# Gathering the tiled products of a linear-attention block: fewer tiled groups, full-array spreads of the reciprocals, scatter pairs, early x loads

## Chip, cores and metric

One core of a Trainium2 chip. The metric is the device time of the kernel in microseconds (us), as the median of several executions. The span that a profile shows is some 1.7 us shorter than that time.

## The reference

Two branches and two residuals are added. x has 2048 tokens of width 640.

```python
xn = layernorm(x)
# branch A: linear attention, 32 heads of width 20
q, k, v = split(xn @ wqkv)
pq, pk  = phi(q), phi(k)              # phi(t) = t+1 if t>0 else exp(t)
kv  = sum over tokens of pk (x) v     # per head, 20 x 20
z   = sum over tokens of pk           # per head
o   = (pq @ kv) / (pq @ z + 1e-6)     # per token and head
A   = o @ wo
# branch B: the 8 tokens of highest x @ w_r go through a gated MLP (640 -> 1536 -> 640);
# the result, times a sigmoid of the score, is added to those 8 rows of x
out = x + A + x + scatter(B)
```

## The kernel before

It first runs over 16 tiles of 128 tokens: layernorm, a transposed copy of the normalised tile (by TensorE for tiles 0 to 3, by a transposing DMA from tile 4 on), the key product K, the phi function, and the Gram product G of the normalised tile with phi(k). Then it turns G into a matrix M = kv·wo (640 x 640), computes the queries in four blocks of 512 tokens, divides them by the denominators, and makes the output tiles as phi(q)/den times M. The routing and the small MLP are threaded between the query products.

What matters for the change is how the small products use TensorE. A product with only 32 output rows is *column-tiled*: four of them, written to four partition ranges of 32, run side by side. A product with only 8 or 32 contraction rows is *row-tiled*: four of them at four partition ranges, written to different PSUM banks, run side by side. All others use the full array. PSUM is one tile of 8 banks, `PS[:, bank, 512]`.

```python
def loads(t):                       # x tiles 6..15, two at a time, on SyncE's DMA queue
    if t < 5:
        ld(sp, XX[:, 6 + 2*t : 8 + 2*t, 1, :], x_v[:, 6 + 2*t : 8 + 2*t, :])
    ...
    # loads(0) follows the first layernorms; loads(1), (2), (3) stand between the transposing
    # DMAs of tiles 4, 5, 6 on the same queue

def m_main(m, b, eng):              # one of 5 slices of M
    for h in range(2):
        for g in range(NG):         # column-tiled, 8 products of 320 columns
            pe.matmul(PS[32*g : 32*g+32, b+h, 0:HW], lhsT=by5(kv1[:, g, :])[:, m, :], rhs=wo1[...], ...)
    for h in range(2):              # full array, 2 products of 320 columns
        pe.matmul(PS[:, b+h, 0:HW], lhsT=by5(kv2[...])[:, m, :], rhs=wo2[...], ...)
    ...                             # copied out by ACT or DVE

def den(tb, bank):                  # denominators of a block: column-tiled, 20 products of 128 columns
    for m in range(KC):
        for j in range(4):
            pe.matmul(PS[32*j : 32*j+32, bank, 0:P], lhsT=zm[:, m, :], rhs=pqT[:, m, ...], ...)
    ...                             # reciprocal as exp(-ln(den)) on ScalarE -> rd

def bcast(tb, b0, js=range(4), n=4):  # spread the reciprocals over the heads' rows: row-tiled (32 rows)
    for j in js:
        pe.matmul(PS[:, b0 + j % n, (j//n)*P : (j//n+1)*P],
                  lhsT=by5(hm[32*j : 32*j+32, :])[:, 0, :], rhs=rd[32*j : 32*j+32, :], ...)
    ...                             # copied to R by ACT

def out_sc(ts):                     # scatter of the MLP result: row-tiled (8 rows), 2 products per output tile
    for t in ts:
        for h in range(2):
            g = 2 * (t % 2) + h
            pe.matmul(PS[:, obank(t)+h, 0:HW], lhsT=OH[32*g : 32*g+8, t*P : (t+1)*P], rhs=ysb[...], start=True, stop=False)

def out_one(t):
    if t < 4:          out_sc((t,))
    elif t % 2 == 0:   out_sc((t, t + 1))
    out_mm(t)                       # 10 full-array products of 320 columns onto the scatter
    out_ev(t)

# ... the middle of the schedule, queries and small groups alternating
m_main(0, 6, dve)
q_pe(1, 1, 0)                       # 5 full-array products of 512 columns
...
m_main(1, 4, act)
den(0, 3)
q_pe(1, 2, 1)
...
```

## Time and profile before

| | |
|---|---|
| time | 123.06 us (122.52 to 123.26 over 4 runs) |
| span of the profile | 121.4 us |
| TensorE from its first query product to its last product (starts) | 56.85 to 117.60: 60.75 us |
| first layernorm step to first query product | 3.61 to 56.85: 53.24 us |

The two last rows cut the kernel at the first query product, and both are measured from start to start. Starts are used because the ends of matmuls are modelled: the Trainium skill says so ("Perfetto Trace Analysis", Tensor Engine Instruction), and this trace shows it, for its matmuls last 0.30 us each and start 0.136 us apart.

The head of the page gives each engine's busy time, its share of the span and its number of instructions:

```profile
span 121.4 us, 2635 instructions
## 1 busy us (share of the span) xinstructions
PE 113.3 (93%) x945; PEld 66.3 (55%) x956; DVE 87.0 (72%) x203; ACT 82.3 (68%) x188; POOL 21.7 (18%) x55
...
```

TensorE ("PE") is the busiest by far. The next view lists for whom TensorE waited: engine and line of the waiter, the releaser, total us, number of times, longest. L198 is K, L175 the transposes of tiles 0 to 3, L118 the warm-up products, L466 the queries.

```profile
...
PE PS L175 <- DVE XX L168: 1.5, 4, 0.5
PE PS L118 <- DVE zero L105: 1.3, 1, 1.3
PE PS L198 <- DMA xnT<-XX: 0.7, 2, 0.5
PE PS L466 <- issue: 0.4, 2, 0.2
```

So TensorE stands still for 1.5 us behind the first layernorms, and 0.7 us in two waits for transposing DMAs. The timeline places those two (start, duration, engine, line, what; in brackets the idle time before and its releaser). These are K of tiles 4, 5 and 6:

```profile
...
20.72 1.54 PE L198 MATMUL PS<-wk,xnT 128*128 128x320 bf16 x10 [0.52 <-DMA xnT<-XX]
...
23.40 1.53 PE L198 MATMUL PS<-wk,xnT 128*128 128x320 bf16 x10
...
26.44 1.54 PE L198 MATMUL PS<-wk,xnT 128*128 128x320 bf16 x10 [0.21 <-DMA xnT<-XX]
...
```

The two gaps of 0.18 us put down to "issue" are no waits: the trace has only 95 of the 100 query records, and each gap is where one of a group of five is missing. After 26.4 us, then, TensorE never stops, so any time to be won from there on is in its own instruction stream. The chain of waits (start, duration, what) shows how that stream spends it. L603 are the column-tiled products of `m_main`, L607 its full-array products, L488 the denominators, L671 the scatter, L680 the output products:

```profile
...
66.00 0.41 PE PS L603 x8
66.41 0.40 PE PS L607 x2
66.81 1.08 PE PS L466 x5
67.89 0.41 PE PS L603 x8
68.29 0.40 PE PS L607 x2
68.69 0.39 PE PS L488 x20
...
102.25 0.25 PE PS L671 x4
102.50 2.83 PE PS L680 x20
...
```

Five queries in a row take 1.08 us, 0.216 each. The eight tiled products of L603 are two waves of 0.136 us, 0.27 us together, yet take 0.41; the two full-array ones behind them would be 0.27 and take 0.40; the 20 output products behind a scatter take 2.83 where 20 x 0.136 is 2.72. Something of the order of 0.1 us is lost at each border between tiled and full-array work. In the whole stretch I counted 27 tiled groups.

In the output stage a spread (L504) and a scatter (L671) often stand next to each other:

```profile
...
93.21 0.25 PE L504 MATMUL PS<-rden,hm 32*128 32x128 bf16 x2
93.22 0.31 PE L671 MATMUL PS<-ysb,tokrow 8*128 8x320 bf16 x2
93.46 1.54 PE L680 MATMUL PS<-Mb,pqT 128*128 128x320 bf16 x10
...
```

Both are row-tiled, and they start 0.01 us apart: the spread runs beside the scatter and costs nothing of its own there.

### The profile page before, as it was taken

How to read it: one execution, taken by the hardware profiler on the slowest of the kernel's cores; microseconds unless marked ns; L12 is line 12 of the kernel's file. 1: busy time of each engine (PE TensorE's matmuls, PEld its weight loads, DVE VectorE, ACT ScalarE, POOL GpSimd, SP SyncE). 2: the span in 40 equal slices, each digit the busy share in tenths (PEclk: the TensorE clock that was granted, in tenths of full speed). 3: DMA queues.
4: the chain of work that ended last, by engine and by line, in shares of the span. 5: the costliest groups of instructions: out<-in, count | busy, mean ns of one | idle time of the engine just before them, and what ended most of it. 6: DMA issues, size and time to landing. Idle time of an engine off the chain costs nothing.

```text
span 121.4 us, 2635 instructions
## 1 busy us (share of the span) xinstructions
PE 113.3 (93%) x945; PEld 66.3 (55%) x956; DVE 87.0 (72%) x203; ACT 82.3 (68%) x188; POOL 21.7 (18%) x55
## 2 busy tenths in 40 slices
PE   5978898999999999999999999999999999999980
PEld 2246554656666666664575444645555565666650
DVE  2699999998999974246777945986596867755540
ACT  4058877778888885547965768889889699990000
POOL 7342243374334431000000033000000000000000
PEclk9999999999999999999999999999999999999999
DMA  3961309993225343899999970000000222322222
GB/s 67 345 188 44 108 7 120 280 250 57 54 59 54 77 80 60 241 376 307 399 400 399 364 273 9 5 3 3 0 5 0 88 74 108 111 105 104 102 103 77
DMA packets 19399, 16.71 MB, mean 138 GB/s; under 512 B 9050, under 2 KB 18106, under 8 KB 19386
## 3 DMA queue, kind: packets, MB, share of 16 engines
q1 hardware_dynamic: 17760, 15.40, 43.5%
q10 hardware_dynamic: 1626, 1.15, 3.2%
q8 instruction: 7, 0.11, 0.4%
q14 instruction: 6, 0.05, 0.1%
HBM read 11.80 MB, written 2.62 MB: 119 GB/s over the span
## 4 chain that ended last, share of the span: by engine, by line
PE 75%; DVE 11%; DMA 6%; POOL 4%; issue 2%; ACT 0%; DVEq 0%
PE PS L680 19%; PE PS L466 18%; PE PS L198 11%; PE PS L229 9%; POOL s L156 4%; DMA xnT<-XX 4%; PE PS L234 3%; DVE XX L168 2%; DVE stats L146 2%; DMA XX<-in_A_x_dram 2%; PE PS L603 2%; PE PS L607 2%; PE PS L671 2%; PE PS L626 1%; PE PS L488 1%
## 5 line engine op out<-in xcount | busy, mean ns | idle before, releaser
L198 PE MATMUL PS<-wk,xnT 128*128 128x320 bf16 (+1 forms) x160 | 24.8, 300 | 1.0 <-DMA xnT<-XX 0.7
L466 PE MATMUL PS<-xnT,wq 128*128 128x512 bf16 x95 | 23.8, 382 | 0.5 <-issue 0.4
L680 PE MATMUL PS<-Mb,pqT 128*128 128x320 bf16 x160 | 23.8, 300 | 0.0
L229 PE MATMUL PS<-pk,XX 128*128 128x512 bf16 x74 | 22.3, 379 | 0.0
L198 PEld LDWEIGHTS <-xnT 128*128 128x128 bf16 x160 | 15.1, 97 | 8.4 <-DMA xnT<-XX 1.4
L216 ACT ACTIVATE ek<-PS 128x320 bf16<-128x320 f32 x32 | 14.1, 442 | 7.7 <-PE PS L198 7.6
L680 PEld LDWEIGHTS <-pqT 128*128 128x128 bf16 x160 | 14.7, 97 | 6.9 <-issue 0.2
L698 DVE TENSOR_TENSOR o<-PS,XX 128x640 bf16<-128x640 f32 x15 | 12.4, 824 | 7.8 <-PE PS L680 7.0
L224 DVE SCALAR_TENSOR_TENSOR pk<-ek,rk 128x640 bf16<-128x640 bf16 x16 | 13.1, 821 | 5.8 <-ACT rk L217 5.6
L472 ACT ACTIVATE qe<-PS 128x512 bf16<-128x512 f32 x20 | 11.9, 595 | 6.5 <-PE PS L466 5.9
L466 PEld LDWEIGHTS <-wq 128*128 128x128 bf16 x100 | 11.0, 120 | 8.2 <-issue 0.6
L478 DVE SCALAR_TENSOR_TENSOR pqT<-qe,qr 128x512 bf16<-128x512 bf16 x20 | 13.5, 685 | 2.4 <-ACT qr L473 2.1
L156 POOL TENSOR_TENSOR s<-t,halfc 128x1 bf16<-128x1 bf16 x16 | 10.1, 632 | 25.0 <-DVE t L155 25.0
L234 PE MATMUL PS<-pk,XX 128*128 128x128 bf16 x64 | 14.0, 219 | 0.3
L217 ACT ACTIVATE rk<-PS 128x320 bf16<-128x320 f32 x32 | 14.2, 445 | 0.0
L191 ACT ACTIVATE XX<-XX,MR,SR 128x640 bf16<-128x640 bf16 x16 | 13.6, 911 | 0.0
L229 PEld LDWEIGHTS <-XX 128*128 128x128 bf16 x80 | 7.8, 98 | 8.4 <-issue 0.3
L473 ACT ACTIVATE qr<-PS 128x512 bf16<-128x512 f32 x20 | 11.8, 592 | 0.0
L158 ACT ACTIVATE c<-XX,MVf 128x640 bf16<-128x640 bf16 x12 | 10.3, 862 | 1.3 <-DVE MVf L147 1.3
L144 DVE BATCH_NORM_STATS2 stats<-XX 128x6 f32<-128x320 bf16 x16 | 7.8, 485 | 1.9 <-DMA XX<-in_A_x_dram 1.9
L146 DVE BATCH_NORM_STATS2 stats<-XX 128x6 f32<-128x320 bf16 x16 | 7.7, 484 | 0.1
L168 DVE TENSOR_SCALAR XX<-c,SR 128x640 bf16<-128x640 bf16 (+2 forms) x17 | 6.6, 395 | 1.4
(132 smaller groups left out, 118.8 us busy)
## 6 DMA issues: line engine op xcount, KB each, us to landing
out_dram<-o SPq DMA_DIRECT2D x15, 160.0 KB, 1.8
wg<-in_B_w_gate_dram SPq DMA_DIRECT2D x5, 384.0 KB, 6.3
wu<-in_B_w_up_dram SPq DMA_DIRECT2D x5, 384.0 KB, 6.8
wd<-in_B_w_down_dram SPq DMA_DIRECT2D x1, 1920.0 KB, 11.3
XX<-in_A_x_dram SPq DMA_DIRECT2D x5, 320.0 KB, 4.0
wk<-in_A_wqkv_dram ACTq DMA_DIRECT2D x2, 400.0 KB, 5.4
wq<-in_A_wqkv_dram SPq DMA_DIRECT2D x1, 800.0 KB, 5.2
wv<-in_A_wqkv_dram SPq DMA_DIRECT2D x1, 800.0 KB, 6.8
```

The lines of the kernel that those rows point to most:

```text
L156: pool.tensor_tensor(out=s[:], in0=t2[:], in1=halfc[:], op=ALU.pow)
L191: act.activation(XX[:, t, 1, :], XX[:, t, 1, :], AF.Identity, bias=MR[:, t : t + 1], scale=SR1[:, t : t + 1])
L198: pe.matmul(PS[:, b + h, 0:w], lhsT=xnT[:, kc, t * P : (t + 1) * P], rhs=wk[:, kc, h * HW : h * HW + w], start=(kc == 0), stop=(kc == KC - 1),
L216: act.activation(ek[:, sl], PS[:, b + h, 0:HW], AF.Exp)
L217: act.activation(rk[:, sl], PS[:, b + h, 0:HW], AF.Relu)
L224: dve.scalar_tensor_tensor(out=pk[:, t, :], in0=ek[:], scalar=1.0, in1=rk[:], op0=ALU.min, op1=ALU.add)
L229: pe.matmul(PS[:, a, :], lhsT=lhsT, rhs=pk[:, t, 0:512], start=(t == 0), stop=(t == T - 1),)
L234: pe.matmul(PS[:, 5, a * P : (a + 1) * P], lhsT=lhsT, rhs=pk[:, t, 512:D], start=(t == 0 and a == 0), stop=(t == T - 1), skip_group_check= ...
L466: pe.matmul(PS[:, bank, :], lhsT=by5(wq[:, kc, :])[:, m, :], rhs=xnT[:, kc, tb * TBLK : (tb + 1) * TBLK], start=(kc == 0), stop=(kc == KC ...
L478: dve.scalar_tensor_tensor(out=pqT[:, m, tb * TBLK : (tb + 1) * TBLK], in0=e, scalar=1.0, in1=r, op0=ALU.min, op1=ALU.add,)
L680: pe.matmul(PS[:, b + h, 0:HW], lhsT=pqT[:, kc, t * P : (t + 1) * P], rhs=Mb[:, kc, h * HW : (h + 1) * HW], start=False, stop=(kc == KC - ...
L698: dve.tensor_tensor(out=ot[:].rearrange("p (h c) -> p h c", h=2), in0=PS[:, b : b + 2, 0:HW], in1=XX[:, t, 1, :].rearrange("p (h c) -> p h ...
```

## The change

Its intent is to cross the border between tiled and full-array work less often. Four parts:

1. **Gathering.** The tiled halves of M's slices go in pairs, and the denominators join other column-tiled groups (the M pair, the gate/up product, the down-projection).
2. **Full-array spreads.** A zero-padded mask (made by GpSimd) turns the row-tiled spread into four full-array products of 128 columns, all into one bank.
3. **Scatter in pairs** also for output tiles 0 to 3.
4. **All x loads early,** ahead of the transposing DMAs; tile 1's centring moves from VectorE to ScalarE.

The diff is shortened: `...` marks cuts, and comments in it are added here.

```diff
+    def consts_g():
+        hm4 = late["hm4"] = st([P, 4, P], BF16, "hm4", "zero")
+        pool.memset(hm4[:], 0.0)
+        for j in range(4):
+            r = slice(32 * j, 32 * j + 32)
+            pool.tensor_copy(hm4[r, j, :], hm[r, :].rearrange("p (q m) -> p m q", m=KC)[:, 0, :])
 ...
-    ln_mid(1, False)
-    consts_e()
+    ln_mid(1)
     ld(act, XX[:, 4:6, 1, :], x_v[:, 4:6, :])
-    loads(0)
+    for t in range(5):
+        loads(t)
+    consts_e()
 ...
-    loads(1)          # after tr_dma(4); likewise loads(2) after tr_dma(5), loads(3) before K(4)
 ...
-    def bcast(tb, b0, js=range(4), n=4):
-        ... row-tiled, over two or four banks ...
+    def bcast(tb, bank):
+        for j in range(4):
+            pe.matmul(PS[:, bank, j * P : (j + 1) * P], lhsT=late["hm4"][:, j, :], rhs=rds[tb][:],
+                      start=True, stop=True, skip_group_check=True)
+        Rs[tb] = tmp.tile([P, 4, P], BF16, tag="R", name="R", bufs=2)
+        act.copy(Rs[tb][:].rearrange("p j c -> p (j c)"), PS[:, bank, :])
 ...
-    m_main(0, 6, dve)
+    m_tiled(0, 6)
+    m_tiled(1, 4)
+    m_full(0, 6, dve)
+    m_full(1, 4, act)
 ...
-    m_main(2, 6, dve)          # and den(0, 3), m_main(3, 4, act) elsewhere
+    m_tiled(2, 6)
+    m_tiled(3, 4)
+    den(0, 3)
+    m_full(2, 6, dve)
+    m_full(3, 4, act)
 ...
+    m_tiled(4, 4)
     gu_pe(6)
+    den(1, 3)
+    m_full(4, 4, dve)
 ...
     y_pe(6)
+    den(2, 3)
 ...
-        if t < 4:
-            out_sc((t,))
-        elif t % 2 == 0:
-            out_sc((t, t + 1))      # now called for pairs from t = 0 on
 ...
```

The changed kernel has the same number of matmuls. Output tiles and spreads use other banks (the spreads bank 3 alone).

More of the change, by code (lines that the diff above doesn't have):

```diff
@@ L298, in consts_c @@
         band(bm1[:], 0, 8)
+    late = {}
+    def consts_g():
[4 more added lines that the diff above has]
+            pool.tensor_copy(hm4[r, j, :], hm[r, :].rearrange("p (q m) -> p m q", m=KC)[:, 0, :])
     def consts_d():
@@ L303 @@
     pool_extra = {3: consts_b, 4: consts_c, 5: consts_d, 6: lambda: tok(0, 512),
-                  7: lambda: tok(512, 1024), 8: lambda: tok(1024, 1536), 9: lambda: tok(1536, S)}
+                  7: lambda: tok(512, 1024), 8: lambda: tok(1024, 1536), 9: lambda: tok(1536, S), 10: consts_g}
     wo_v = A_wo.rearrange("(g r) d -> r g d", r=GC)
@@ L334 @@
     ln_stats(1, 1)
-    ln_mid(1, False)
+    ln_mid(1)
+    ld(act, XX[:, 4:6, 1, :], x_v[:, 4:6, :])
+    for t in range(5):
+        loads(t)
     consts_e()
-    ld(act, XX[:, 4:6, 1, :], x_v[:, 4:6, :])
-    loads(0)
     K(0, (0,), 4)
@@ L386 @@
     tr_dma(5)
-    loads(2)
     PHa(3)
@@ L393 @@
     G(2)
-    loads(3)
     for t in range(4, T):
@@ L410 @@
             pool_extra[t - 1]()
-        loads(t)
+        if t > 4:
+            loads(t)
     corner_ts = list(range(T - 1))
@@ L492, in den, with den_ev @@
                 )
+    def den_ev(tb, bank):
         ld_ = tmp.tile([P, P], F32, tag="lden", name="lden")
@@ L499 @@
     Rs = {}
-    def bcast(tb, b0, js=range(4), n=4):
-        rd = rds[tb]
-        for j in js:
-            pe.matmul(
-                PS[:, b0 + j % n, (j // n) * P : (j // n + 1) * P], lhsT=by5(hm[32 * j : 32 * j + 32, :])[:, 0, :],
-                rhs=rd[32 * j : 32 * j + 32, :],
-                start=True, stop=True, skip_group_check=True,
-            )
-        if tb not in Rs:
-            Rs[tb] = tmp.tile([P, 4, P], BF16, tag="R", name="R", bufs=2)
-        R = Rs[tb]
-        j0, j1 = js[0], js[-1] + 1
-        if n == 4:
-            act.copy(R[:], PS[:, b0 : b0 + 4, 0:P])
-        else:
-            act.copy(R[:, j0:j1, :], PS[:, b0 : b0 + n, (j0 // n) * P : (j0 // n + 1) * P])
+    def bcast(tb, bank):
[4 more added lines that the diff above has]
+        act.copy(Rs[tb][:].rearrange("p j c -> p (j c)"), PS[:, bank, :])
     def norm(tb, h0, h1):
@@ L598, in kv_ev, with m_tiled @@
                           in1=bm2[:], op=ALU.mult)
-    def m_main(m, b, eng):
+    def m_tiled(m, b):
         for h in range(2):
@@ L605, in m_main, with m_full @@
                           start=True, stop=False, skip_group_check=True)
+    def m_full(m, b, eng):
         for h in range(2):
@@ L628, in gu_pe, with gu_act @@
                               start=(kc == 0), stop=(kc == KC - 1), skip_group_check=True)
+    def gu_act(b):
         act.activation(hf[0][:], PS[:, b, P:512], AF.Exp, scale=-1.0)
@@ L649, in y_pe, with y_ev @@
                               start=(k == 0), stop=(k == 2), skip_group_check=True)
+    def y_ev(b):
         src = PS[:, b : b + 2, P : P + HW]
@@ L661, in ysum @@
                           scalar1=cols[:, 1:2], scalar2=None, op0=ALU.mult)
+    OB = [6, 4, 0, 6, 4, 0, 6, 4] + [0, 2, 6, 4] * 2
     def obank(i):
-        return (6, 2, 0)[i % 3] if i < 8 else (4, 0, 2, 6)[i % 4]
+        return OB[i]
     def out_sc(ts):
@@ L733 @@
     q_fin(1, 0)
-    m_main(1, 4, act)
-    den(0, 3)
     q_pe(1, 2, 1)
     q_fin(1, 1)
-    m_main(2, 6, dve)
+    m_tiled(2, 6)
[3 more added lines that the diff above has]
+    m_full(3, 4, act)
+    den_ev(0, 3)
     q_pe(1, 3, 2)
@@ L741 @@
     gates()
-    m_main(3, 4, act)
     q_pe(1, 4, 0)
     q_fin(1, 3)
-    m_main(4, 6, dve)
     q_pe(2, 0, 1)
     q_fin(1, 4)
-    route3(3)
-    bcast(0, 4)
+    route3(5)
+    bcast(0, 3)
     q_pe(2, 1, 2)
     q_fin(2, 0)
+    norm(0, 0, 2)
+    m_tiled(4, 4)
     gu_pe(6)
-    norm(0, 0, 2)
+    den(1, 3)
+    m_full(4, 4, dve)
+    gu_act(6)
+    den_ev(1, 3)
     q_pe(2, 2, 0)
     q_fin(2, 1)
-    den(1, 3)
     norm(0, 2, 4)
@@ L761 @@
     q_pe(2, 4, 2)
-    ht_pe(3)
+    bcast(1, 3)
+    ht_pe(4)
     q_fin(2, 3)
-    bcast(1, 4, (0, 1), 2)
     q_pe(3, 0, 0)
@@ L767 @@
     y_pe(6)
-    bcast(1, 4, (2, 3), 2)
+    den(2, 3)
+    y_ev(6)
+    den_ev(2, 3)
+    norm(1, 0, 2)
     q_pe(3, 1, 1)
-    norm(1, 0, 2)
     q_fin(3, 0)
@@ L777 @@
     q_fin(3, 2)
-    den(2, 3)
+    bcast(2, 3)
+    xpx(0)
     q_pe(3, 4, 1)
     q_fin(3, 3)
-    xpx(0)
+    out_sc((0, 1))
+    out_one(0)
     q_fin(3, 4)
-    norm(1, 2, 4)
-    out_one(0)
-    bcast(2, 4, (0, 1), 2)
     xpx(1)
     out_one(1)
-    bcast(2, 4, (2, 3), 2)
+    norm(1, 2, 4)
+    den(3, 2)
+    den_ev(3, 2)
     norm(2, 0, 2)
     xpx(2)
+    out_sc((2, 3))
     out_one(2)
-    den(3, 3)
     norm(2, 2, 4)
+    bcast(3, 3)
     xpx(3)
@@ L797 @@
     out_one(3)
-    bcast(3, 4, (0, 1), 2)
+    norm(3, 0, 2)
     xpx(5)
+    out_sc((4, 5))
     out_one(4)
-    bcast(3, 4, (2, 3), 2)
-    norm(3, 0, 2)
+    norm(3, 2, 4)
     xpx(6)
     out_one(5)
-    norm(3, 2, 4)
     for t in range(7, T):
@@ L808 @@
     for t in range(6, T):
+        if t % 2 == 0:
+            out_sc((t, t + 1))
         out_one(t)
```

## The prediction

> **What bounds it.** TensorE. The page gives it 113.3 of 121.4 us busy, and the timeline shows it without a gap from 26.4 us to its last matmul at 117.9; granted clock 1.00 throughout. Before 22 us the chain of waits runs through VectorE's layernorm steps. The list of waits gives TensorE only 0.7 us behind the transposing DMAs (0.52 at 20.2 us, 0.21 at 26.2), 1.5 us behind the first layernorms and 1.3 at the start.
>
> **Where TensorE loses time.** From the first query product (56.9) to the end (117.9) is 61.0 us. Summing the matmuls at the cadence the trace shows (512 columns 0.216, 320 columns 0.136, 128 columns 0.056 us, tiled products four side by side) gives 54.4 us. The missing 6.6 us sit at the borders of the tiled groups: full-array queries that follow a tiled group start 1.20 us apart per five instead of 1.08; a tiled group of eight 320-column products takes 0.41 where two waves need 0.27; a scatter group takes 0.25 where one wave needs 0.136, and the 20 products behind it 2.83 for 2.72. I count 27 tiled groups, so about 0.245 us each. The Trainium skill, "TensorEngine Tiling (Array Packing)", Key Properties, says that changing the tiling mode drains the engine; the numbers agree.
>
> **What changes.**
> - Tiled groups: the five kv-by-wo groups become three, two of them shared with a denominator group and one with gate/up; down-projection and denominators share one; the reciprocal spreads leave the row-tiled mode; the first four scatters go in pairs. 27 groups become 15: estimate 12 x 0.245 = -2.9 us.
> - Two scatter waves fewer: -0.27 us.
> - Spreads at full array: 16 x 0.056 = 0.90 us; before they cost about 0.37, since several ran beside a scatter: +0.5 us.
> - x loads early: the transposes took 3.8 and 4.3 us to land beside x loads, 2.7 as median. The two DMA waits should go: -0.7 us. Moving one centring to ScalarE gains nothing: VectorE then waits for GpSimd's power (ends 8.3 us).
> - GpSimd gets some 2 us (the spread mask), in a gap of 2.1 us between its power steps at 42 to 44.6 us: off the path.
> - New waits: the last denominators need the last query block, whose VectorE step now stands behind the first output: about +0.25 us. In the middle, ScalarE gets longer runs (gate/up 1.6 us plus denominator 0.7) before the next query; three query banks should hide it. Allow +0.3 us for waits unforeseen.
>
> All of these TensorE terms are on the critical path. Sum about -2.8 us; the 3.5 us after the last matmul stay.
>
> **Prediction: 120.2 us**, 8 in 10 between 119.3 and 121.6. Faster by over 2% (below 120.57): 0.62; within 2%: 0.36; slower by over 2%: 0.02.
>
> **Right if:** TensorE's time from first query to last matmul falls from 61.0 to about 58.8; kv-by-wo groups of 16 take about 0.68 us and the full ones behind them 0.67; the scatter pairs 0.25 each, eight of them; spreads 0.22 to 0.25 in one run of four; K of tiles 4 and 6 no longer wait for a DMA; the transposes land in 2.7 us; VectorE's and ScalarE's busy time nearly unchanged.
>
> **Wrong if:** the border cost depends on what is switched, not on the number of groups (a tiled-to-tiled change costs too, or each weight load of a full spread shows); early x loads delay the key weights, or tiles 4 and 5 needed at 12.3 us, so that the layernorm chain starts late; ScalarE or VectorE, working in order, becomes the wait around the merged gate/up group (75 to 85 us) or at the last denominators (92 us), because TensorE now arrives there earlier. Each would show as idle TensorE with that releaser.

## The result, and the profile after

The changed kernel took **120.02 us** (119.93 to 120.16 over 4 runs) against 123.06 us. The ratio is 0.9755, 95% interval 0.9723 to 0.9787. Ratios here are the mean time of one kernel's fast runs over that of the other's in the same rounds, so they are not quite the ratio of the medians. Executions over 1.5% slower than the fastest of the same kernel are left out of the means.

```profile
span 118.4 us, 2647 instructions
## 1 busy us (share of the span) xinstructions
PE 111.8 (94%) x956; PEld 67.8 (57%) x956; DVE 85.9 (73%) x202; ACT 82.7 (70%) x186; POOL 23.8 (20%) x60
...
```

```profile
...
PE PS L118 <- DVE zero L105: 1.3, 1, 1.3
PE PS L175 <- DVE XX L168: 1.1, 3, 0.5
PE PS L198 <- DMA xnT<-XX: 0.5, 1, 0.5
```

In the changed kernel the lines have moved: L474 is the query, L603 and L609 the tiled and full-array halves of M, L496 the denominators, L679 the scatter, L688 the output; L198, L175 and L118 are as before. Its chain of waits in the same places:

```profile
...
65.17 0.68 PE PS L603 x16
65.85 0.67 PE PS L609 x4
66.53 2.16 PE PS L474 x10
68.68 0.68 PE PS L603 x16
69.36 0.28 PE PS L496 x20
69.64 0.67 PE PS L609 x4
...
92.43 0.46 PE PS L496 x20
92.89 0.25 PE PS L679 x4
...
```

Sixteen tiled products take 0.68 us where twice eight took 0.82, the full-array ones behind them 0.67 where they took 0.80, and 20 denominator products inside a tiled group take 0.28, exactly five waves of 0.056, where they took 0.39 alone. The last denominators (at 92.43) take 0.46 instead of 0.39: this is the new wait behind the last query block.

K of tiles 4, 5 and 6 in the timeline after:

```profile
...
20.28 1.54 PE L198 MATMUL PS<-wk,xnT 128*128 128x320 bf16 x10 [0.45 <-DMA xnT<-XX]
...
22.96 1.53 PE L198 MATMUL PS<-wk,xnT 128*128 128x320 bf16 x10
...
25.62 1.53 PE L198 MATMUL PS<-wk,xnT 128*128 128x320 bf16 x10
...
```

The wait of tile 6 is gone: it starts 2.66 us after tile 5, before it was 3.04. The wait of tile 4 is still there, 0.45 us after 0.52. The time from issue to landing of the 12 transposing DMAs, before and then after:

```profile
...
DMA to landing us min/median/max: 2.6/2.7/4.3
```

```profile
...
DMA to landing us min/median/max: 2.6/2.6/3.7
```

The longest fell from 4.3 us (tile 6, beside x loads) to 3.7. That 3.7 is tile 4's, issued at 16.48 us and waited for until 20.23 us, with no x load left in flight.

Cut at the first query product, the result is:

| | before | after | difference |
|---|---|---|---|
| first layernorm step to first query | 53.24 | 52.71 | -0.53 |
| first query to last product | 60.75 | 58.60 | -2.15 |

The remaining 0.30 us of the two profiles' distance is the landing of the first x tile (3.61 and 3.31 us), which no part of the change touches.

### The profile page after: what moved, and what is told of

The parts are those of the page before. It is cut to its first block, busy times and chain, and to the rows that moved or that the text cites. A ratio compares the mean times of both kernels' runs of the same rounds, so it can differ in the third digit from the quotient of the medians.

```text
span 118.4 us, 2647 instructions
## 1 busy us (share of the span) xinstructions
PE 111.8 (94%) x956; PEld 67.8 (57%) x956; DVE 85.9 (73%) x202; ACT 82.7 (70%) x186; POOL 23.8 (20%) x60
## 4 chain that ended last, share of the span: by engine, by line
PE 80%; DVE 8%; DMA 5%; POOL 3%; issue 1%; ACT 0%; DVEq 0%
PE PS L688 19%; PE PS L474 19%; PE PS L198 14%; PE PS L229 12%; DMA xnT<-XX 3%; POOL s L156 3%; PE PS L234 2%; DMA XX<-in_A_x_dram 2%; DVE XX L168 2%; DVE stats L146 2%; PE PS L679 2%; PE PS L603 1%; PE PS L609 1%; PE PS L628 1%; PE PS L585 1%; PE PS L496 1%
## 5 line engine op out<-in xcount | busy, mean ns | idle before, releaser
L198 PE MATMUL PS<-wk,xnT 128*128 128x320 bf16 (+1 forms) x160 | 24.8, 300 | 0.7 <-DMA xnT<-XX 0.5
L474 PE MATMUL PS<-xnT,wq 128*128 128x512 bf16 x100 | 23.6, 380 | 0.0
L688 PE MATMUL PS<-Mb,pqT 128*128 128x320 bf16 x160 | 23.5, 299 | 0.0
L229 PE MATMUL PS<-pk,XX 128*128 128x512 bf16 x80 | 23.3, 379 | 0.0
L198 PEld LDWEIGHTS <-xnT 128*128 128x128 bf16 x160 | 15.2, 97 | 7.9 <-DMA xnT<-XX 0.8
L688 PEld LDWEIGHTS <-pqT 128*128 128x128 bf16 x160 | 14.9, 97 | 6.7
L474 PEld LDWEIGHTS <-wq 128*128 128x128 bf16 x100 | 11.3, 118 | 8.3 <-issue 0.3
L158 ACT ACTIVATE c<-XX,MVf 128x640 bf16<-128x640 bf16 x13 | 11.2, 859 | 1.3 <-DVE MVf L147 1.3
L559 POOL COPY xsT<-xnT 128x5 bf16 x8 | 2.5, 308 | 26.6 <-ACT qr L481 24.0
```

The source lines that it names most:

```text
L198: pe.matmul(PS[:, b + h, 0:w], lhsT=xnT[:, kc, t * P : (t + 1) * P], rhs=wk[:, kc, h * HW : h * HW + w], start=(kc == 0), stop=(kc == KC - 1),
L229: pe.matmul(PS[:, a, :], lhsT=lhsT, rhs=pk[:, t, 0:512], start=(t == 0), stop=(t == T - 1),)
L474: pe.matmul(PS[:, bank, :], lhsT=by5(wq[:, kc, :])[:, m, :], rhs=xnT[:, kc, tb * TBLK : (tb + 1) * TBLK], start=(kc == 0), stop=(kc == KC ...
L688: pe.matmul(PS[:, b + h, 0:HW], lhsT=pqT[:, kc, t * P : (t + 1) * P], rhs=Mb[:, kc, h * HW : (h + 1) * HW], start=False, stop=(kc == KC - ...
```

## Experiments

The theory: time is lost per *border* between tiled and full-array work, and the 2.15 us come from having fewer groups; the early loads add the rest. The rivals: the loss is per small product and not per border; the full-array spread, or the loads, carry the gain; the parts are independent.

### The border by itself: four probes in the changed kernel

Each probe puts 15 small products of 32 columns, whose result nothing reads, into spare PSUM columns between the two halves of output tiles 0 to 14. Only the kind and the grouping differ; the results stay correct.

```diff
+    def probe(t, n=1):
+        for _ in range(n):
+            # p_full: lhsT = pqT[:, 0, 128 columns]  -> PS[:, b, 320:352]
+            # p_col, p_col3: lhsT = zm[:, 0, :] (32)  -> PS[0:32, b, 320:352]
+            # p_row:  lhsT = OH[8 rows, 128 columns]  -> PS[:, b, 320:352]
+            pe.matmul(...)
     ...
     for h in range(2):
         for kc in range(KC): ...
+        if h == 0 and not last: probe(t)            # p_full, p_col, p_row
+        if h == 0 and t in (4, 8, 12): probe(t, 5)  # p_col3
```

`p_full`: 

> Changed kernel plus 15 small full-array products (32 columns) put between the two halves of the first 15 output tiles; results unused. Theory (each border between full-array and tiled work costs about 0.12 us): no border here, so only each product's own slot, 0.03 to 0.06 us: +0.4 to +0.9 us on the changed kernel's 120.0. Rival (any extra small product or weight load on TensorE costs about a quarter of a us there): +3.5 us.

`p_col`: 

> The same 15 places, but each product is column-tiled (32 of 128 output rows, 32 columns). Theory: each is a tiled group of its own with two borders, 0.245 us, and 0.02 to 0.05 of its own: +3.9 us (3.4 to 4.5) on the changed kernel's 120.0. Rival (cost per product, not per border): the same as the full-array ones, within 0.3 us.

`p_row`: 

> The same 15 places, each product row-tiled (8 contraction rows, as in the output scatter). Theory, if the border does not care which way the array is split: +3.9 us (3.4 to 4.5), as the column-tiled ones. If only column tiling carries the border: +0.4 to +0.9.

`p_col3`: 

> 15 column-tiled products again, but five in a row at three places. Theory (cost per group): 3 x 0.245 plus 15 slots of 0.03 to 0.06 = +1.2 to +1.6 us. Rival (cost per tiled product): the same as with 15 places, about +3.9.

| run | time, us | first query to last product | against the changed kernel's 58.60 |
|---|---|---|---|
| p_full | 120.69 | 58.96 | +0.36: 0.024 per product |
| p_col | 123.07 | 61.91 | +3.31: 0.221 per product |
| p_row | 123.42 | 61.89 | +3.29: 0.219 per product |
| p_col3 | 121.13 | 59.59 | +0.99 |

The timeline of the column-tiled probe (L699 the probe, L688 the output products), then of the full-array probe:

```profile
...
101.19 1.53 PE L688 MATMUL PS<-Mb,pqT 128*128 128x320 bf16 x10
102.65 0.19 PE L699 MATMUL PS<-pqT,zm 128*32 128x32 bf16 x1
102.78 0.85 PE L688 MATMUL PS<-Mb,pqT 128*128 128x320 bf16 x5
...
```

```profile
...
98.80 0.18 PE L699 MATMUL PS<-Mb,pqT 128*128 128x32 bf16 x1
98.83 0.84 PE L688 MATMUL PS<-Mb,pqT 128*128 128x320 bf16 x5
...
```

The tiled probe starts 1.46 us after ten products (ten at 0.136 are 1.36), and the next product starts 0.13 us after it; the full-array one is followed after 0.03 us. A visit to tiled work and back therefore costs 0.221 - 0.024 = 0.197 us, both ways of tiling alike. Five tiled products in one place pay it once: 3 x 0.197 + 15 x 0.024 is 0.95 us, measured 0.99. The rival, a cost per small or per tiled product, is out. My expectation of +3.9 us was too high by 0.6: a visit for one small product costs 0.20 us and not 0.245.

The kernel's own visits cost somewhat more. By the starts, in the kernel before, a scatter pair costs 0.22 us (the 20 products before it take 0.11 too long, its own wave 0.11), and a slice of M 0.26 (five queries before it take 1.17 instead of 1.08, its eight tiled products 0.41 instead of 0.27, the two full-array ones 0.30 instead of 0.27). A direct change from column to row tiling costs about 0.1 us as well. These are the down-projection and the tiled products behind it, before (row-tiled spread) and after (column-tiled denominators):

```profile
...
84.88 1.00 PE L647 MATMUL PS<-wd,hT 128*32 128x320 bf16 x24
85.81 0.25 PE L504 MATMUL PS<-rden,hm 32*128 32x128 bf16 x2
...
```

```profile
...
82.86 1.00 PE L651 MATMUL PS<-wd,hT 128*32 128x320 bf16 x24
83.69 0.45 PE L496 MATMUL PS<-pqT,zm 128*32 128x128 bf16 x20
...
```

The six waves of the down-projection are 0.82 us. The next product starts after 0.83 where the tiling stays the same, and after 0.93 where it changes. (The last denominators before a scatter show it too: 0.39 us to the scatter's start, for 0.28.) So each change of mode counts, and not each group. The 24 visits before, two of them with a direct change, are 50 changes; the 14 visits after, one of them with a direct change, are 29. An estimate from the figures above is 0.12 us per change.

The Trainium skill ("TensorEngine Tiling (Array Packing)", Key Properties) says: "Changing tiling mode (not just tile) drains the TensorE". The probes agree and put 0.197 us on the round trip. The skill ("TensorE: Matmul & The Clock Gate", "Wait — 56ns, not 53.3ns?") also says that matmuls never start less than about 25 ns apart, however small; the full-array probe's 24 ns agrees. Tiled products side by side start closer: the spread and the scatter shown above are 0.01 us apart.

### The parts alone, on the kernel before

Early loads alone (`b_loads`): the load lines of the diff above, with the moved centring. 

> Before plus the early x loads alone (and the one centring moved to ScalarE, as in the change). My reading of the changed kernel: only the wait of tile 6 for its transposing DMA goes, with what it drags, some 0.4 us; the wait of tile 4 (0.45 to 0.5 us) stays, because the first transposing DMA takes 3.7 us to land with nothing else in flight. So -0.4 us (-0.2 to -0.6), 122.6. The prediction's version: both waits go, -0.7. Rival (the gain is mostly the loads): -1.5 or more.

Gathering alone (`b_group`): the schedule lines for M and for the denominators of blocks 0 to 2, with the old row-tiled spreads and single scatters. 

> Before plus the gathering of tiled groups alone: kv-by-wo in three groups, denominators of blocks 0, 1, 2 joined to other tiled groups, spreads and scatters as before. Six groups fewer at 0.245 us: -1.5 us (-1.1 to -1.8), 121.6. Rival (the full-array spreads or the loads carry the gain): within 0.4 us of before.

Full-array spreads alone (`b_spread`): the mask and the new `bcast`, one call per block where the first of the two old calls stood. 

> Before plus the full-array spread of the reciprocals alone, one run of four products per block, GpSimd's mask included. Three tiled groups fewer (-0.65 us) against full-array products that no longer hide beside the scatters (+0.6 us): 0 (-0.3 to +0.2). Rival (full-array spreads carry the gain): -1 us or more.

Scatter pairs alone (`b_pairs`):

```diff
-        if t < 4:
-            out_sc((t,))
-        elif t % 2 == 0:
+        if t % 2 == 0:
             out_sc((t, t + 1))
```

> Before plus the scatter pairs for the first four output tiles alone. The spreads of block 2, which shared a row-tiled group with a scatter, now stand alone, so only one group and one scatter wave go: -0.3 us (0 to -0.5). If pairs and spreads were independent, two groups and two waves: -0.75.

| run | time, us | ratio to before (95%) | first query to last product (before 60.75) |
|---|---|---|---|
| b_loads | 122.13 | 0.9922 (0.9892 to 0.9953) | 60.76 |
| b_group | 121.95 | 0.9900 (0.9874 to 0.9925) | 59.85: -0.90 |
| b_spread | 122.94 | 0.9985 (0.9960 to 1.0011) | 60.69: -0.06 |
| b_pairs | 122.82 | 0.9976 (0.9947 to 1.0005) | 60.55: -0.20 |

The spreads and the pairs did what was expected of them: nothing, and 0.2 us. No single part carries the gain.

The gathering missed in the stretch: -0.90 us and not -1.5. (The time alone would not have shown it: by the ratio it fell by 0.9 to 1.55 us.) Its timeline shows two waits (L466 query, L605 the tiled product of M's last slice, L641 VectorE's gating of the MLP, L646 the transposes of what L641 writes):

```profile
...
74.52 1.27 PE L466 MATMUL PS<-xnT,wq 128*128 128x512 bf16 x5
76.07 0.48 PE L605 MATMUL PS<-wo,kv 128*32 128x320 bf16 x8 [0.28 <-ACT R L516]
...
78.90 3.18 PE L466 MATMUL PS<-xnT,wq 128*128 128x512 bf16 x14
...
81.55 0.56 DVE L641 TENSOR_TENSOR hh<-PS,hh 128x384 bf16<-128x384 f32 x1
...
82.16 0.17 PEld L646 LDWEIGHTS <-hh 128*128 128x128 bf16 x3 [0.55 <-DVE hh L641]
82.16 0.34 PE L646 MATMUL PS<-ident,hh 128*128 128x128 bf16 x3
...
```

TensorE first waits for ScalarE. The profile counts 0.28 us from the modelled end of the queries; by the starts the five queries take 1.55 us where they take 1.17 before M's other slices, so the wait costs 0.38. The old spread writes banks 4 to 7, and M's gathered slice, which now comes soon after it, needs bank 4; ScalarE must first copy the spread out. The second wait is not in the list of TensorE's waits, because the modelled ends of the queries hide it; it shows at the weight load ("PEld") of the transposes. The 14 recorded queries at 0.216 us are done at 81.92, and the transposes start at 82.16, when VectorE has finished. That costs 0.24. Without both waits the six groups fewer would have given 1.52 us, the 1.5 that were expected: 0.127 us for each of 12 changes of mode.

The loads missed the other way: 0.96 us as the ratio gives it (0.0078 of 123; 0.6 to 1.3 by its interval), where I expected 0.4.

### Parts together

`a_oldloads` is the changed kernel with the loads of before. 

> The changed kernel with the x loads (and the one centring) where before had them: all of the TensorE regrouping, none of the early loads. If loads and regrouping add up: the stretch from first query product to last matmul stays at the changed kernel's 58.6 us (before 60.75), and the first query comes 0.5 us later after the first layernorm step than in the changed kernel (53.2 instead of 52.7): 120.6 us (120.3 to 121.1), ratio to before 0.980. Rival (the loads are worth the 0.9 us that the loads-alone run showed): 121.0 or more.

`b_group_spread` is `a_oldloads` that also takes the scatter pairs of tiles 0 to 3 apart again. 

> Gathered groups and full-array spreads together, with the old loads and with the first four scatters one by one. Theory: the gathering alone lost 0.28 us to a wait for ScalarE, since the old spread and the gathered product meet in one bank; the one-bank spread takes that wait away, so the two together are worth more than their sum (0.90 + 0.06 us in the stretch from first query to last matmul): 59.3 us there (-1.45), 121.5 in all. Rival (parts independent): 59.8, 122.0.

`b_spread_pairs` is `b_spread` and `b_pairs` together. 

> Before plus full-array spreads plus scatter pairs. Alone they moved the stretch from first query to last matmul by -0.06 and -0.20 us. Theory: a spread that rode in a scatter's group needs both to go before the group goes; together five groups vanish against 0.6 us of added full-array products: -0.5 us (-0.35 to -0.7) in the stretch, 122.4 in all. Rival (independent): -0.26.

| run | time, us | ratio to before (95%) | first query to last product (before 60.75) | sum of the parts alone |
|---|---|---|---|---|
| a_oldloads | 120.88 | 0.9827 (0.9808 to 0.9845) | 58.60: -2.15 | -1.16 |
| b_group_spread | 121.61 | 0.9881 (0.9863 to 0.9900) | 59.21: -1.54 | -0.96 |
| b_spread_pairs | 122.64 | 0.9973 (0.9948 to 0.9998) | 60.27: -0.48 | -0.26 |

The parts are not independent. Alone they add up to 1.16 us, together they give 2.15. Gathering and spreads together show neither of the two waits (0.38 and 0.24 us): the one-bank spread leaves bank 4 alone, and the spread of block 1 now stands in front of the MLP's transposes. That is about what the two together give beyond their sum (1.54 against 0.96). Spreads and pairs together remove the groups in which a spread rode beside a scatter; each alone leaves that group standing for the other one. (The times of the last row agree, within their interval, with the 0.5 us.)

The stretch of `a_oldloads` is the changed kernel's to the hundredth, so the loads act on the front alone. Their worth is again about 0.9 us: 120.88 against 120.02 us, in different jobs; by the ratios to before, 0.9827 - 0.9755 = 0.0072, 0.89 us. The time of 120.88 lies inside what I had expected (120.3 to 121.1), towards the rival's 121.0; the 0.9 us are what the rival said.

### Where the loads' 0.9 us are

Seven kernels have the old loads and seven the early ones. The profile of each shows where K of tiles 4, 5 and 6 starts.

| | old loads (7 profiles) | early loads (7 profiles) |
|---|---|---|
| tile 5's K to tile 6's K | 3.04 to 3.93, mean 3.42 | 2.66 to 2.68, mean 2.67 |
| first layernorm step to tile 4's K | 16.61 to 17.28, mean 17.02 | 16.62 to 17.12, mean 16.86 |
| longest landing of a transposing DMA | 4.3 to 4.9 | 3.4 to 3.9 |
| first layernorm step to first query | 53.19 to 54.00, mean 53.55 | 52.36 to 52.86, mean 52.60 |

0.75 of the 0.95 us are tile 6's wait. The kernel before, in the one profile that the prediction was read from, happened to show the mildest case of all seven, 3.04. The harshest is `a_oldloads`:

```profile
...
22.88 1.54 PE L198 MATMUL PS<-wk,xnT 128*128 128x320 bf16 x10
...
26.81 1.54 PE L198 MATMUL PS<-wk,xnT 128*128 128x320 bf16 x10 [1.09 <-DMA xnT<-XX]
...
```

Tile 4's start moves by 0.16 us in the mean, and the two ranges overlap: the early loads did not take its wait away.

### Why tile 4's transposing DMA is slow

It is the first transposing DMA of the program. If the first were slow as such, one spent early on a scratch buffer would cure it (`a_first`):

```diff
     for t in range(5):
         loads(t)
+    sp.dma_start_transpose(Gs[:, :, 0:P], XX[:, 0, 0, :])   # Gs is overwritten later
     consts_e()
```

> The changed kernel with one more transposing DMA, of the first normalised tile into a scratch buffer, issued right behind the x loads at about 9 us; nothing reads it. Theory (only the first transposing DMA of the program is slow, 3.7 us to landing against 2.6): the wait of tile 4 (0.45 us) goes: 119.6 us, 0.4 below the changed kernel; the transposing DMA of tile 4 lands in 2.6 to 2.7. Rival (tile 4's is slow for another reason, such as being the first after a quiet stretch, or its data): no change, landing 3.7.

It took 119.88 us (119.59 to 120.11), ratio to before 0.9742 (0.9719 to 0.9764). The landing times of the 12 working transposing DMAs:

```profile
...
DMA to landing us min/median/max: 2.6/2.6/3.5
```

Tile 4's still took 3.5 us (issued at 16.57, K at 20.08 after a wait of 0.16), inside the range that the kernels with early loads and without this line show (3.4 to 3.9). The time is not distinguishable from the changed kernel's either. (The added one, queued behind the x loads, took 6.3 us to land.) So my theory falls, and why this DMA takes 0.8 to 1.3 us longer than the usual 2.6 stays open. Two candidates that no run tells apart: it is the first after some 2 us in which the DMA engines moved nothing, or something in the data's path to it. This kernel is not claimed to be better than the changed one.

## Why the prediction was right

Predicted 120.2 us, measured 120.02. The mechanism was right; several terms were off, and their errors nearly cancelled.

| term of the sum | predicted | what the runs showed |
|---|---|---|
| 12 tiled groups fewer | 12 x 0.245 = -2.9 | 21 changes of mode fewer, the worth of 10.5 visits, at 0.12: -2.5 |
| two scatter waves fewer | -0.27 | not measured by itself |
| spreads at full array | +0.5 | b_spread: 5 changes fewer at 0.12 and a net of -0.06 leave +0.54 |
| last denominators behind the first output | +0.25 | 0.46 instead of 0.39 us: +0.07 |
| unforeseen waits | +0.3 | none found after 26 us |
| **first query to last product** | **-2.1** | **-2.15** |
| x loads early | -0.7 | -0.9 |

- **The groups were over-counted.** 27 less 15 is 12, but the trace shows 10.5 visits' worth of changes fewer. The 0.245 per group came out near what the kernel's own visits cost, and that was luck: all 6.6 us that the stretch lost were divided by the same too large count, and the loss also holds other things, such as the four one-column products that spread the chosen rows (0.53 us where they stand alone). The probe, with one small product, gives 0.197; why it is below the kernel's visits stays open. The prediction named a tiled-to-tiled change that costs as a sign against itself. There is such a cost, about 0.1 us, but only two such changes stood in the kernel before and one in the changed one.
- **The waits were over-sized.** No new wait appeared around the merged gate/up group. `b_group` shows that this fear was not idle: with the old spread there are two, of ScalarE and of VectorE, and with the change's own spreads neither shows.
- **The step of the loads was half wrong.** "The two DMA waits should go: -0.7 us": only tile 6's went. Tile 4's DMA is slow without any x load beside it. That the size came out near is luck: tile 6's wait is worth 0.75 us on average, more than the single profile of before showed.
- **GpSimd's mask** took 2.1 us (0.52 and 1.54) between 41.6 and 43.7 us, in the gap between two power steps, and TensorE did not wait, as foreseen. The moved centring gained no time that stands out from the spread, as foreseen.
- "K of tiles 4 and 6 no longer wait" as a sign in the profile was right for tile 6 and wrong for tile 4. The other signs came: 0.68, 0.67, eight scatter pairs of 0.25, spreads of 0.22 in runs of four (0.33 for the one behind the row-tiled routing columns).

## What to carry to other kernels

Count changes of tiling mode and not tiled products: a visit to tiled work and back cost 0.20 to 0.26 us here whichever way the array was tiled, and a change from column to row tiling 0.1. So put tiled products of one kind that can wait next to each other. Measure waits by starts: modelled ends hid one of 0.24 us. Before removing one member of a mixed group, see whether the group stays for the other members: the spreads and the pairs gave 0.06 and 0.20 us alone, and 0.48 together, and a part that is worth nothing alone (the full-array spread) can be what keeps another part from waiting. A wait behind a DMA read from one profile is one draw from a wide range (0.4 to 1.3 us beyond the even cadence here); look at several before sizing its removal.

## What the Trainium skill lacked or had wrong

- "TensorEngine Tiling (Array Packing)", Key Properties, has that a change of tiling mode drains the engine, and gives no cost. Here: 0.197 us for a probe's visit to tiled work and back, the same for column tiling (61.91 us) and row tiling (61.89 us); up to 0.26 for the kernel's own visits, and about 0.1 for a direct change from column to row tiling.
- No page that I read says that a transposing DMA can be slow with no other load in flight: tile 4's took 3.4 to 3.9 us to land where most took 2.6. The cause is open.
- The 25 ns floor between small matmuls ("TensorE: Matmul & The Clock Gate") is stated there without an exception. It showed as 24 ns between full-array products, but not between tiled ones side by side: the spread and the scatter shown above start 0.01 us apart. Nothing else was found that contradicts what these pages state.
